# Backward recurrence of a memory-augmented attention: dO of a segment in four column groups over 32 rows, the other 8 rows batched by token tile

## The chip, the cores and the metric

One core of one Trainium2 chip. The metric is the time of one execution on the device in microseconds (us). The kernel before takes 3108.94 us (median of 3 runs, 3106.38 to 3111.91).

## The reference, cut to what matters

A pre-norm block: attention with a recurrent memory, then a gated feed-forward (FFN). The kernel computes the output and nine gradients. The attention works through the 2048 tokens in 64 segments of 32; each segment sees 8 memory rows ahead of its tokens, and the first 8 rows of its output are the memory of the next segment.

```python
M, seg = 8, 32; H, Dh, Dm = 16, 256, 448; n_seg = 2048 // 32
mem = mem0
for s in range(n_seg):
    h = concatenate([mem, x[:, s*seg:(s+1)*seg]])          # 40 rows
    q, k, v = h @ Wq, h @ Wk, h @ Wv                       # 16 heads of 256
    p = softmax(where(mask, q @ k.T * Dh**-0.5, -1e9))
    o = (p @ v) @ Wo                                       # 40 x 448
    mem = o[:, :M]; outs.append(o[:, M:])
```

The backward pass runs through the segments from the last to the first. The gradient of the 8 output rows that became memory comes from the segment handled just before. So for each segment the order is fixed: dO = do x Wo^T (40 rows, 4096 columns), dP = dO x V^T, the softmax gradient dS, the gradients of the heads (dV from P and dO, dK and dQ from dS), their projections back to 448 columns, and the fold that adds the four partial sums and gives the next 8 rows. Of the 40 rows of `do`, only the 8 memory rows wait for the segment before. The change makes two groups of them: 32 rows (the memory rows and 24 token rows) that go through the chain, and the 8 other token rows, which are known long before. Four segments form a token tile of 128 tokens.

Of the kernel before, what the change touches and what calls it, by code (L numbers as in the profile page):

```python
# [812 lines left out]
def ffn_phase(k: _K, back):  # L813
# [32 lines left out]
    for i in range(2):  # L846
        nc.gpsimd.memset(dhb_b[i][:, D:DP], 0.0)
# [88 lines left out]
    for n, gi in enumerate(turns):  # L936
# [67 lines left out]
        for tt in range(G):  # L1004
# [16 lines left out]
            nc.scalar.copy(out=dh_b[:, 0:D], in_=dh_t)  # L1021
            nc.gpsimd.dma_start(out=dr["DHb"][rows, :], in_=dh_b)
# [9 lines left out]
def backward_chain(k: _K):  # L1032
# [9 lines left out]
    WoT_sb = W(0, KC, HD)  # L1042
# [7 lines left out]
    dO_sb = A(52, 16, P)  # L1050
    doT = A(56, 32, 64)
# [5 lines left out]
    P_bd, dS_bd, dST_bd = [B(1.25 * i, 8, 2, L) for i in range(3)]  # L1057
# [13 lines left out]
    def load_seg(s):  # L1071
        if s < NSEG - 1:
            load_v(s)
        for w, (nm, T_sb) in enumerate((("q", Q_sb), ("k", K_sb))):
            t1 = dr["T1"][s, :, w].rearrange("(g x i) n -> g i x n", g=2, x=2)
            t0 = dr["T0" + nm][s // 8].rearrange("(x s i) (g n) -> s g i x n", x=2, s=8, g=2)
            for g in range(2):
                for src, i0, i1 in ((t1[g], M, L), (t0[s % 8, g], 0, M)):
                    k.last_load = nc.sync.dma_start(out=T_sb[64 * g + i0:64 * g + i1].rearrange("p (x c) n -> p x (c n)", x=2), in_=src)
        P_sb = Pb[s % 2]  # L1080
        with tc.issue_after(k.pool_op.ins) if s == NSEG - 1 else nullcontext():
            nc.gpsimd.dma_start(out=P_sb.rearrange("p h n -> p (h n)"), in_=dr["P_all"][s])
        for g in range(2):
            pool_op = nc.gpsimd.tensor_copy(out=P_bd[64 * g:64 * g + L, :, g, :], in_=P_sb[64 * g:64 * g + L, :, :])
        stores("mid", s, pool_op.ins)
# [12 lines left out]
    for tl in (Q_sb, K_sb, P_bd, dS_bd):  # L1098
        nc.gpsimd.memset(tl, 0.0)
    nc.gpsimd.memset(do_roll[:, :, (NSEG - 1) % NWIN, SEG:L], 0.0)  # L1100
    prep_tile(NT - 1)
    load_seg(NSEG - 1)
    load_v(NSEG - 1)
    nc.sync.dma_start(out=WkT_sb[:, 2:MC], in_=dr["Tk"][:, 2:MC])
    yield
    nc.sync.dma_start(out=WoT_sb[:, 0:3, :], in_=dr["To"][:, 0:3, :])
    nc.sync.dma_start(out=WoT_sb[0:64, 3, :], in_=dr["To"][0:64, 3, :])
    nc.gpsimd.memset(WoT_sb[64:P, 3, :], 0.0)
# [5 lines left out]
    nc.vector.memset(doT[:, :, L:64], 0.0)  # L1114
    nc.gpsimd.memset(dST_bd, 0.0)
    nc.gpsimd.memset(dxT[:, KC - 1, :], 0.0)
    om = k.f32("f1", DP, "omb")
    nc.gpsimd.memset(om[:], 0.0)
# [5 lines left out]
    def head_mm(ps, lhs, rhs_bd, turned):  # L1124
        for cl in range(16):
            b, i = divmod(cl, 6)
            at = 8 * (cl // 4 % 2) + 4 * (cl // 8) + cl % 4 if turned else cl
# [3 lines left out]
    for s in range(NSEG - 1, -1, -1):  # L1131
# [7 lines left out]
        if r == 2:  # L1139
            prep_tile(t - 1)  # L1140
        if s < NSEG - 1:
            load_seg(s)

        with k.prio.crit():
            pss = [k.ps1() for _ in range(4)]
            for j in range(MC):
                c = cj(j)
                b, jj = divmod(j, 8)
                for kc in range(KC):
                    with tc.issue_after(k.last_dh.ins) if s == NSEG - 1 and j == 0 and kc == 0 else nullcontext():  # L1150
                        nc.tensor.matmul(pss[b][:, jj * L:(jj + 1) * L], lhsT=WoT_sb[:, kc, c * P:(c + 1) * P],  # L1151
                                         rhs=do_roll[:, kc, sl, :], start=(kc == 0), stop=(kc == KC - 1))
            for b in range(4):
                k.evac(doT[:, 8 * b:8 * b + 8, 0:L], pss[b][:, 0:8 * L].rearrange("p (c n) -> p c n", n=L), "vsvs"[b])

            def token_major(hf):
                ph = k.ps1()[:].bitcast(BF16)
                for i in range(8):
                    c0 = 2 * (8 * hf + i)
                    nc.tensor.transpose(ph[:, i * P:(i + 1) * P], doT[:, c0:c0 + 2, :].rearrange("p c n -> p (c n)"), ident[:, :])  # L1160
                nc.scalar.copy(out=dO_sb[:, 8 * hf:8 * hf + 8, :], in_=ph.rearrange("p (c n) -> p c n", n=P))  # L1161
            token_major(0)
            token_major(1)
            pD = k.ps1()
            for h in range(8):
                for g in range(2):
                    for dc in range(DC):
                        j = 2 * (2 * h + dc) + g
                        nc.tensor.matmul(pD[64 * g:64 * g + 64, h * L:(h + 1) * L], lhsT=doT[:, j, :], rhs=vT[:, 2 * h + dc, L * g:L * g + L],
                                         start=(dc == 0), stop=(dc == DC - 1), skip_group_check=True)  # L1170
# [10 lines left out]
            nc.vector.tensor_tensor(out=dS_bd, in0=prod.unsqueeze(2).to_broadcast([P, 8, 2, L]), in1=P_bd, op=ALU.mult)  # L1181
# [3 lines left out]
            def heads(nm, lhs, rhs):  # L1185
                pps[nm] = [k.ps1() for _ in range(3)]
                head_mm(pps[nm], lhs, rhs, nm != "v")
# [6 lines left out]
                if s == 0:  # L1194
                    k.tl.outs(*{"v": (7, 9), "k": (9, 10), "q": (10, 11)}[nm], 0, 6)
# [7 lines left out]
            heads("v", dO_sb, P_bd)  # L1203
# [12 lines left out]
            rows_in("k", WkT_sb, 20, MC)  # L1216
            rows_in("q", WqT_sb, 0, MC)
            k.last_om = nc.vector.tensor_copy(out=om[:, 0:224], in_=pH[:, 0:224])
            nc.scalar.copy(out=om[:, 224:D], in_=pH[:, 224:D])
            pm = k.ps1()  # L1220
            for kc in range(KC):
                nc.tensor.matmul(pm[:, kc * 32:(kc + 1) * 32], lhsT=om[:, kc * P:(kc + 1) * P], rhs=sel[:],  # L1222
                                 start=True, stop=True)
            pm3 = pm[:, 0:KC * 32].rearrange("p (c m) -> p c m", m=32)
# [291 lines left out]
```

## The kernel before: what the change touches

`k.prio.crit()` marks instructions that belong to the recurrence. The order on each engine is fixed when the program is built: among the instructions that could go, those marked come first, and everything else (from here on: the filler) goes where none of those is ready. `k.ps1()` gives one of five PSUM banks, `k.fx1()` one of two that the filler uses, `k.evac(out, in, "v" or "s")` copies from PSUM on DVE or ACT.

```python
# backward_chain, for s from 63 to 0; t, r = divmod(s, 4)
with k.prio.crit():
    pss = [k.ps1() for _ in range(4)]
    for j in range(MC):                                  # MC = 32 column blocks
        for kc in range(KC):                             # KC = 4, the last padded with zeros
            matmul(pss[b][:, jj*L:(jj+1)*L], lhsT=WoT_sb[:, kc, c*P:(c+1)*P],   # 128 x 128
                   rhs=do_roll[:, kc, sl, :], ...)                              # 40 columns
    for b in range(4): k.evac(doT[:, 8*b:8*b+8, 0:L], pss[b]..., "vsvs"[b])
    token_major(0); token_major(1)                       # 8 transposes and one ACT copy each: dO_sb
    # dP: 32 matmuls, then the softmax gradient on DVE
    nc.vector.scalar_tensor_tensor(out=prod, in0=pD3, scalar=k.scale, in1=P_sb, ...)
    nc.vector.tensor_reduce(out=rsum[:], in_=prod, ...)
    nc.vector.scalar_tensor_tensor(out=prod, in0=pD3, scalar=k.scale, in1=rsum..., ...)
    nc.vector.tensor_tensor(out=dS_bd, in0=prod..., in1=P_bd, op=ALU.mult)
    heads("v", dO_sb, P_bd);  rows_in("v", WvT_sb, 0, MC)   # 16 matmuls of 80 columns; 32 of 448
    heads("k", Q_sb, dS_bd)
    # 16 matmuls that turn dS
    rows_in("k", WkT_sb, 0, 20);  heads("q", K_sb, dST_bd)
    rows_in("k", WkT_sb, 20, MC); rows_in("q", WqT_sb, 0, MC)
    # fold: om = pH; pm = om x sel; do_roll[next] = pm[..., 24:32]
    ...
if r == 0:                                               # once per tile: filler
    px = k.fx1()
    for wi, (nm, WT) in enumerate((("q", WqT_sb), ("k", WkT_sb), ("v", WvT_sb))):
        for j in range(MC): matmul(px[32*(j%4):...], lhsT=lo[nm][:, j, :], rhs=WT[:, cj(j), :], ...)
    # copied, folded into pl = k.fx1(), turned in pX = k.fx1(), layer norm backward, stored
```

## Time and profile before

| stage | stretch (us) | what it is |
|---|---|---|
| forward | 0 to 1055 | not touched |
| FFN backward | 1055 to 1358 | small extra copies only |
| start of the chain | 1358 to 1383 | its first segment, behind a store |
| backward chain | 1383 to 2395 | 63 segments, the change |
| tail | 2395 to 3104 | weight gradients, not touched |

The prediction below shows how the stage is read.

I name a tile's segments r3, r2, r1, r0 in the order in which they run. The four segments between these two copies, from r0 to r1 of the next tile, take 65.46 us. Over the 14 tiles after the first the medians are r3 16.12, r2 16.04, r1 17.04 and r0 15.83, and the tile's is 65.03. The very first tile, which has no filler of an earlier tile beside it, takes 65.05.

### The profile page before, as it was taken

The page shows a single profiled execution, that of the slowest core. Times are in us where ns is not written, and L with a number is a line of the kernel's source. Part 1 is how long each engine was busy: PE and PEld are TensorE (multiplying, and loading weights), DVE is VectorE, ACT ScalarE, POOL GpSimd, SP SyncE. Part 2 cuts the span into 40 slices and gives each one's busy share as a digit, 9 for nine tenths or more (in the row PEclk, how much of TensorE's full clock was granted, in tenths as well). Part 3 has the DMA queues.
Part 4 walks back from the last instruction along what each step waited for, and adds up shares of the span by engine and source line. Part 5 has one row for each costly group of instructions (what it writes and reads, how often), then busy time and mean ns, then how long its engine had stood idle before and what let it go on. Part 6 is the DMA issues. An engine that isn't in the chain of part 4 may idle for free.

```text
span 3103.7 us, 108341 instructions
## 1 busy us (share of the span) xinstructions
PE 2914.8 (94%) x47640; PEld 1735.5 (56%) x47650; DVE 1331.6 (43%) x3381; ACT 1112.6 (36%) x2634; POOL 674.7 (22%) x1511
## 2 busy tenths in 40 slices
PE   5899999989988999989999999999999899999998
PEld 3555555545544555666666666666666454444443
DVE  3555455455455576654444444544445101111110
ACT  2444344344444544443434344444344001111110
POOL 2222222222222222321122111221211111212111
PEclk9999999999999999999999999999999899999999
DMA  6567756756756899984455445555544999969951
GB/s 242 136 172 178 183 162 167 191 158 167 189 161 182 276 222 228 221 298 119 133 150 143 128 137 142 143 139 136 141 138 133 284 267 244 190 181 199 192 160 57
DMA packets 739084, 550.12 MB, mean 177 GB/s; under 512 B 600052, under 2 KB 634852, under 8 KB 736180
## 3 DMA queue, kind: packets, MB, share of 16 engines
q1 hardware_dynamic: 687380, 389.19, 51.5%
q0 software_dynamic: 51232, 154.00, 14.9%
q8 instruction: 374, 6.13, 0.8%
q14 instruction: 98, 0.80, 0.1%
HBM read 168.01 MB, written 234.23 MB: 130 GB/s over the span
## 4 chain that ended last, share of the span: by engine, by line
PE 72%; issue 11%; DVE 6%; DMA 5%; ACT 4%; POOL 2%; SPq 1%; ACTq 0%; POOLq 0%; DVEq 0%
PE po L1200 7%; PE psf L1151 7%; PE psf L535 6%; PE psf L652 5%; PE po L697 4%; PE psf L1375 4%; PE psf L890 4%; PE psf L1128 4%; PE psf L1396 4%; PE fx L1264 3%; PE fx L1014 3%; PE fx L464 2%; PE psf L1222 2%; DVE arA L75 2%; PE psf L549 2%
## 5 line engine op out<-in xcount | busy, mean ns | idle before, releaser
L75 DVE CAST arA<-psf 128x256 bf16<-128x256 f32 (+3 forms) x933 | 427.2, 480 | 808.6 <-PE psf L1375 275.2
L76 ACT CAST arA<-psf 128x96 bf16<-128x96 f32 (+5 forms) x915 | 352.4, 409 | 1036.6 <-PE psf L1375 261.2
L1200 PE MATMUL po<-arW,arA 128*32 128x448 bf16 x6144 | 347.3, 355 | 4.6 <-DMA arW<-Tq 3.5
L1375 PE MATMUL psf<-arW,arA 128*128 128x512 bf16 x980 | 247.1, 380 | 0.0
L1375 PEld LDWEIGHTS <-arA 128*128 128x128 bf16 x1440 | 136.0, 98 | 164.8 <-issue 13.8
L1151 PEld LDWEIGHTS <-arW 128*128 128x128 bf16 x8192 | 213.4, 96 | 25.0 <-issue 25.0
L1151 PE MATMUL psf<-arA,arW 128*128 128x40 bf16 x8192 | 217.0, 180 | 6.2 <-DVE arA L1226 5.1
L652 PE MATMUL psf<-arW,arA 128*64 128x512 bf16 x1536 | 219.0, 386 | 0.0
L1200 PEld LDWEIGHTS <-arA 128*32 128x32 bf16 x6144 | 152.0, 96 | 115.8 <-ACT arA L76 9.4
L535 PE MATMUL psf<-arW,arA 128*32 128x512 bf16 x3072 | 193.8, 385 | 12.5 <-DVE arA L738 12.5
L76 ACT CAST arB<-psf 128x64 bf16<-128x64 f32 (+3 forms) x384 | 121.8, 318 | 153.1 <-PE psf L539 109.7
L697 PE MATMUL po<-arW,arA 128*32 128x256 bf16 (+1 forms) x4096 | 144.2, 267 | 10.5 <-DVE arA L75 7.5
L890 PE MATMUL psf<-arW 128*128 128x256 bf16 (+1 forms) x1288 | 146.3, 274 | 1.3 <-DVE arA L956 0.7
L890 PEld LDWEIGHTS <-arW 128*128 128x128 bf16 (+1 forms) x1344 | 102.4, 97 | 51.4 <-issue 40.8
L1161 ACT COPY arA<-psf 128x1024 bf16<-128x1024 bf16 x128 | 123.3, 1015 | 2.2 <-PE psf L1160 0.4
L1128 PEld LDWEIGHTS <-arW 128*128 128x128 bf16 x2048 | 86.4, 99 | 61.8 <-issue 56.9
L535 PEld LDWEIGHTS <-arA 128*32 128x32 bf16 x3072 | 70.6, 97 | 90.0 <-DVE arA L738 18.1
L76 ACT COPY arA<-psf 128x512 bf16<-128x512 bf16 (+3 forms) x142 | 84.3, 594 | 99.9 <-DVE arA L75 90.3
L464 PE MATMUL fx<-arA,arW 128*128 128x64 bf16 (+1 forms) x2048 | 84.3, 196 | 32.4 <-ACT arB L76 19.2
L697 PEld LDWEIGHTS <-arA 128*32 128x32 bf16 x4096 | 95.9, 98 | 32.9 <-DVE arA L75 10.5
L1128 PE MATMUL psf<-arB,arW 128*128 128x80 bf16 x2048 | 96.8, 201 | 13.6 <-DVE arB L1181 5.2
L1436 POOL DMA_DIRECT2D out_dram<-arA x96 | 51.7, 546 | 249.7 <-DVE arA L75 246.9
(290 smaller groups left out, 4645.7 us busy)
## 6 DMA issues: line engine op xcount, KB each, us to landing
arW<-T SPq DMA_DIRECT2D x256, 128.0 KB
X_o<-arA SPq DMA_DIRECT2D x37, 512.0 KB
T<-arA SPq DMA_DIRECT2D x64, 256.0 KB
X_v<-arA POOLq DMA_DIRECT2D x32, 512.0 KB, 4.9
X_k<-arA POOLq DMA_DIRECT2D x32, 512.0 KB, 4.0
X_q<-arA POOLq DMA_DIRECT2D x32, 512.0 KB, 3.1
out_dram<-arA POOLq DMA_DIRECT2D x90, 128.0 KB, 3.5
VG<-arA SPq DMA_DIRECT2D x64, 160.0 KB
```

What stands on the lines that cost most here:

```text
L75: return nc.vector.tensor_copy(out=out, in_=in_)
L76: return nc.scalar.copy(out=out, in_=in_)
L464: nc.tensor.matmul(banks[w][:, i * 64:(i + 1) * 64], lhsT=lhsT, rhs=xr[lo:hi, kc, :], start=(kc == 0 and i == 0), stop=(kc == KC - 1), ski ...
L535: nc.tensor.matmul(banks[w][32 * q:32 * q + 32, :], lhsT=hT_roll[:, kc, sl, M:L], rhs=(Wq_sb, Wk_sb)[w][:, kc, col(q, b)], start=(kc == 0) ...
L652: nc.tensor.matmul(pV[b][64 * g:64 * g + 64, 0:512], lhsT=hT_flat[:, kc, sl * L:sl * L + 64], rhs=Wv_sb[:, kc, n * 512:(n + 1) * 512], sta ...
L697: nc.tensor.matmul(pO[32 * q:32 * q + 32, 0:w], lhsT=xblk[:, j, r * SEG:(r + 1) * SEG], rhs=Wo_sb[:, cj(j), 256 * dh:256 * dh + w], start= ...
L890: nc.tensor.matmul(ps[fp][:, f2 * 256:(f2 + 1) * 256], lhsT=Wt[lo:hi, kc, c * P:(c + 1) * P], rhs=xT[lo:hi, kc, :], start=(kc == 0 and f2 ...
L1128: nc.tensor.matmul(ps[b][:, i * 2 * L:(i + 1) * 2 * L], lhsT=lhs[:, at, :], rhs=rhs_bd[:, cl // 2, :, :].rearrange("p g n -> p (g n)"), st ...
L1151: nc.tensor.matmul(pss[b][:, jj * L:(jj + 1) * L], lhsT=WoT_sb[:, kc, c * P:(c + 1) * P], rhs=do_roll[:, kc, sl, :], start=(kc == 0), stop ...
L1200: nc.tensor.matmul(pH[32 * (j % 4):32 * (j % 4) + 32, 0:D], lhsT=blk[nm][:, j, r * SEG:(r + 1) * SEG], rhs=WT[:, cj(j), :], start=(nm == " ...
L1375: nc.tensor.matmul(pa[2 * kc + g][:, 0:w], lhsT=lhs_of(b)[:, kc * P:(kc + 1) * P], rhs=rhs_of(b, g), start=(b == 0), stop=(b == nblk - 1), ...
L1396: k.last_mm = nc.tensor.matmul(pa[i][:, 0:D], lhsT=lhs_of(b, i), rhs=rhs_of(b), start=(bi == 0), stop=(bi == len(nblk) - 1))
```

## The change

dO was computed transposed, 40 columns at a time: 128 short matmuls at the floor of about 26 ns each. Now the 32 rows of the chain are the stationary operand, and 512 columns of Wo stream past them, in four groups of 32 array columns at once. dO comes out token-major in two banks and needs 8 transposes instead of 16. The price: Wo's last 64 rows are packed in halves and taken with 64x32 matmuls; P must be laid out by column group (8 matmuls and two DVE products per segment); the V heads (now ahead of dP) take two operands of 160 columns, the second one for the 8 other rows; and those 8 rows are computed for a whole tile in four "units" of 32 matmuls, issued in segments r2 and r1 of the tile handled before, ranked with the chain, each with both filler banks.

```diff
 with k.prio.crit():
-    for j in range(MC):
-        for kc in range(KC):
-            matmul(pss[b][:, jj*L:(jj+1)*L], lhsT=WoT_sb[:, kc, c*P:(c+1)*P], rhs=do_roll[:, kc, sl, :], ...)
-    token_major(0); token_major(1)
+    banks = [k.ps1(), k.ps1()]
+    for b in range(2):
+        for kc in range(KC - 1):
+            for q in range(4):
+                matmul(banks[b][32*q:32*q+32, :], lhsT=do_roll[:, kc, sl, M:L], rhs=WoT_sb[:, kc, col(q, b)], ...)
+        for q in range(4):
+            g, x = divmod(q, 2)
+            matmul(banks[b][32*q:32*q+32, :], lhsT=do_roll[64*x:64*x+64, KC-1, sl, M:L],
+                   rhs=WoT3[64*x:64*x+64, (2*g+b)*512:(2*g+b+1)*512], ...)
+        k.evac(dO_sb[:, b, :], banks[b][:], "vs"[b])
+    turned(0)                       # 4 transposes, evicted into doT
+    values(1)                       # V heads, 8 matmuls: the other 8 rows (dO_rest)
+    turned(1)
+    values(0)                       # V heads, 8 matmuls: the 32 rows (dO_sb)
     ... dP, softmax gradient
-    heads("v", dO_sb, P_bd)
     rows_in("v", WvT_sb, 0, MC)
     ... K heads, Q heads, projections
+    if s > 0: p_by_groups(s - 1)    # 8 matmuls, 2 DVE products with the group mask
     rows_in("q", WqT_sb, 0, MC)
+    if t > 0:
+        for u in {2: (0, 1), 1: (2, 3)}.get(r, ()): rest_unit(t - 1, u)
+        if r == 0: rest_turned(t - 1)
     ... fold
+def rest_unit(t, u):                # 8 other rows of a tile's four segments: 32 columns
+    banks = [k.fx1(), k.fx1()]
+    for kc, i, g, x in ...:         # 32 matmuls
+        matmul(banks[x][:, ...], lhsT=WoT_sb[:, kc, c*P:(c+1)*P],        # kc = 3: 64 rows of WoT3
+               rhs=do_roll[lo:hi, kc, s0:s0+4, 0:M], ...)
```

Cut: buffer addresses, loads, start-up, the fold of the last 64 columns to both halves, evictions of the V heads, the last step of dS in two operations.

## The prediction

> **What bounds the kernel now.** I first read the table of busy time by stretch, to find the stage that the change touches. It is the backward chain: 64 segments, one after the other, each of which needs 8 memory rows from the one before.
>
> ```profile
> 0.00:1055.00 1055.00, 945.81 (x17935) 521.45 (x17936) 542.36 (x1641) 442.00 (x1101) 258.71 (x705) 0.98 0.66 178
> 1055.00:1358.00 303.00, 298.43 (x2278) 183.30 (x2277) 209.67 (x338) 145.17 (x275) 88.91 (x121) 1.00 0.95 252
> 1383.00:2395.00 1012.00, 973.62 (x22959) 696.53 (x22959) 478.39 (x1216) 415.96 (x1082) 198.46 (x458) 1.00 0.50 137
> ```
>
> The columns are the stretch, its length, and busy us of PE, PE weight load, DVE, ACT and POOL. The third row holds 63 segments: 1012 / 63 = 16.06 us each, a third of the kernel. PE looks 96% busy, DVE 47%, the DMA share is 0.50. But the busy figure of PE counts every matmul's whole latency, so it doesn't say whether PE's rate or the order of the dependences sets these 16.06 us. For that I read the chain that ended last through one segment in which PE had almost no other work to put in between:
>
> ```profile
> 2068.86 3.35 PE psf L1151 x128
> 2072.22 0.94 PE psf L1160 x16
> 2073.16 0.64 PE psf L1169 x32
> 2073.80 0.02 issue
> 2073.82 0.49 DVE prod L1176
> 2074.32 0.46 DVE arA L75
> 2074.78 0.39 DVE rsum L1178
> ...
> 2075.18 0.42 DVE arA L75
> 2075.61 0.40 DVE prod L1179
> 2076.01 0.06 DVE arA L75
> ...
> 2076.11 0.84 DVE arB L1181
> ...
> 2077.08 0.39 PE psf L1128 x6
> ...
> 2079.50 0.73 PE psf L1128 x16
> ...
> 2084.90 0.13 PE psf L1151
> ```
>
> Start, length, what. The segment runs from 2068.86 to 2084.90, 16.04 us, in four parts: A, 4.96 us: dO by 128 matmuls, 16 transposes, dP by 32 matmuls. B, 3.26 us: the softmax gradient on DVE, into which three evictions of the V heads (L75: 0.46, 0.42, 0.06) have slipped. C, 2.42 us: K heads and the turning of dS. D, 5.40 us: Q heads, the last projections, the fold to the 8 rows. The segment before, with a dozen and more filler matmuls of L1264 (the memory-row projections of a token tile), took 16.03 us too. So the chain of dependences is the bound, and filler lies free in its gaps.
>
> How near is PE's rate? From the lengths of dense runs in the time order: L1151 128 in 3.30 us (26 ns each), L1160 16 in 0.97 (61), L1169 32 in 0.64, heads 16 in 0.75, L1200 43 in 2.2 (51), turning of dS 0.36, fold (L1222) 1.05. A segment's own work is 3.30 + 0.97 + 0.64 + 3 x 0.75 + 96 x 0.051 (4.9) + 0.36 + 1.05 = 13.5 us. Filler is, per tile of four segments, 96 x 0.051 = 4.9 for L1264 and about 1.8 for folding and turning it: 1.7 per segment. Sum 15.2 of 16.06 us. PE is thus only 0.9 us per segment behind the chain, and this caps the gain.
>
> **What the Trainium skill says.** "TensorE: Matmul & The Clock Gate", Part 3 (Packing small matmuls): outputs at partitions 32j of PSUM land in distinct column groups and run concurrently, three such tiles 2.38 times as fast. The trace agrees: the forward chain's L535 has this very form, and 24 of them take 1.41 us, 59 ns each at 512 columns, where one latency is 385 ns. The same page, Part 1 ("Wait — 56ns, not 53.3ns?"): warm start-to-start is N / 2.4 GHz + 2.5 ns and never below about 25 ns. L1151's 26 ns for 40 columns is that floor, so 40 columns waste it; that is what the change attacks, and the 32-column matmuls that it adds stay on it. "TensorEngine Tiling (Array Packing)", PSUM Bottleneck, warns that eviction may become the limit once tiling has sped up PE. That bears on part A, where eviction of 512 columns is new:
>
> ```profile
> L535 PE MATMUL psf<-arW,arA 128*32 128x512 bf16 x3072 | 193.8, 385 | 12.5 <-DVE arA L738 12.5
> L76 ACT COPY arA<-psf 128x512 bf16<-128x512 bf16 x128 | 74.9, 585 | 88.5 <-DVE arA L75 88.5
> L75 DVE CAST arA<-psf 128x512 bf16<-128x512 f32 x96 | 66.2, 689 | 89.3 <-PE psf L539 87.0 <-PE psf L660 2.1
> L75 DVE COPY arA<-psf 128x512 bf16<-128x512 bf16 x128 | 53.7, 419 | 52.8 <-PE psf L549 52.8
> ```
>
> (Groups of the forward chain: count, busy us, mean ns, idle before.) Evictions to come will cost 0.69 us on DVE from fp32, 0.42 from bf16, 0.585 on ACT.
>
> **The change, part by part: PE work per segment.** dO: out go 128 matmuls (3.30), in come 24 of 128x32 at 59 ns and 8 of 64x32, guessed at 60: 1.89. Transposes: 16 (0.97) become 8 (0.49). V heads: 16 of 80 columns (0.75) become 16 of 160 columns, because P is split by column group and the other 8 rows come from a second operand; 160 / 2.4 + 2.5 = 69 ns by the page's rule, but 80 columns measure 46 against the rule's 36, so I take 75: 1.2. P by groups: 8 in four column groups, 0.2. The other 8 rows: per tile 128 matmuls at the 26 ns floor (3.3) and 8 transposes (0.5), 0.95 per segment. Fold: two more passes, 0.05. Change: -1.41 - 0.48 + 0.45 + 0.2 + 0.95 + 0.05 = -0.24. PE work falls only from 15.2 to 14.95 us: most of what the column groups save is spent again.
>
> The chain of dependences. Part A: dO 1.89; the first half turned (0.25) and half of the V heads (0.6, from the rows known beforehand) cover the ACT eviction of the second half, which ends 1.89 + 0.06 + 0.585 + 0.06 = 2.6 us in; turning the second half until 3.0; its ACT eviction until 3.7 lies beside the other V heads (until 3.6); dP starts there and ends at 4.25. Before: 4.96, gain 0.7. Part B: the V evictions of the high rows start ahead of dP, so 0.46 + 0.42 leave the softmax chain and about 0.2 (low rows) stays; dS becomes two operations of 320 elements, about 0.4 each by L1178/L1179, so the same 0.84. B is 3.26 - 0.75 = 2.5. C and D stay at 2.4 and 5.4, at best. The chain is then about 14.55 us.
>
> Now the two bounds have changed places: the chain would allow 14.55, PE needs 14.95. The gaps in the chain (14.55 less its own PE work of 12.3 = 2.25 us) are smaller than the filler (1.7 + 0.95 = 2.65). No schedule fills gaps fully: with filler to spare, segments before were still at 16.1 for 15.2-15.5 us of work. I add 0.5 us of unfilled time: 15.45 us. Gain 16.06 - 15.45 = 0.6 us, times 63 = 38 us.
>
> Elsewhere: 128 matmuls, evictions and the first P operand (some 6 us) come ahead of the first segment. That segment sits for 11.7 us behind a DMA store (DGP, in the chain of waits at 1367), and I expect the new work to hide there. The extra 64-column copies in the FFN stage (16 x about 0.2 us of ACT) are beside a PE that is 98% busy. P_bd's two POOL copies (0.45 us each) go, a POOL copy of 256 columns comes; POOL is 20% busy. The tail stays.
>
> **The rivals.** First: PE's rate doesn't bind because my dense rates are too high and the packing is good; then the chain's 14.55 to 14.95 decides, and the gain is 1.1 to 1.5 us per segment, 70 to 95 us (3015 to 3040). For it: before, filler was free. Against: 96% PE busy and filler that outgrows the gaps. Second: a tile's filler becomes a chain of its own. L1264's projection, its fold and the 8-row units share two PSUM banks, each unit takes both and waits for its evictions, and the next tile's dP and V heads can't start without the units. L1264's filler took from 2016.6 to 2061, nearly three segments, with gaps of 2.5 us; with smaller gaps it may take four, and the chain then stalls at each tile's boundary by some 3 to 7 us, eating the gain: 3090 to 3110. Third: DVE's order. The new products of P with the group mask are 640 elements from PSUM, 0.82 us each by L1181, twice per segment. If such a one starts just before an operation of the chain, the chain waits, as it does now for the V evictions. Twice 0.5 us would take the chain back to 15.5 and give a gain of 20 to 35 us (3075 to 3090). For it: a DVE that goes from 47% to about 60% of the time. Fourth: the gain is nil because DMA loads set the pace; a DMA share of 0.50 and hardly any wait of the chain on DMA speak against it.
>
> **Range and chances.** My centre is 3108.94 - 38 = 3071 and the first rival pulls a little lower: 3069. The range goes from nearly full packing (15.0 us per segment, -67 us) to most of the gain lost (15.9, -10): 3042 to 3098. More than 2% needs 62 us, or 15.07 us per segment, only 0.12 above the PE work I count; I give it 0.22. Slower by 2% would need stalls of 5 us per tile on top of no gain: 0.03.
>
> **What would show it right or wrong.** In the new profile the chain should run at about 15.4 us per segment with PE busy still at 95% or more; the dO matmuls should take about 1.9 us per segment, and the time from the first dO matmul to the end of dP 4.2 to 4.5; the softmax part 2.3 to 2.6; DVE near 60%. Filler that still runs in every segment, with the last segment of a tile no shorter than the others, would confirm PE's rate as the bound. It is wrong if segments take 15.0 us or less (packing better than I hold possible), if the first segment of each tile is several us longer than the others (second rival), or if the DVE products of P stand in the chain that ended last (third).

## More of the kernel before

One view is added here, since it measures every kernel that follows: each segment ends with one small DVE copy (L1226) that writes the 8 rows for the next, so the distance of two such copies is the length of a segment. They are from the time order of DVE in the kernel before, over one token tile; the columns are start, length, engine, line, operation, and in brackets the idle time before it and what ended it.

```profile
2003.15 0.19 DVE L1226 CAST arA<-psf 128x32 bf16<-128x32 f32 x1 [1.58 <-PE psf L1222]
...
2068.61 0.19 DVE L1226 CAST arA<-psf 128x32 bf16<-128x32 f32 x1 [1.58 <-PE psf L1222]
```

## The result, and the profile after

After: 3137.72 us (median of 4 runs, 3135.56 to 3150.49), beside 3109.4 for the kernel before (4 runs). A ratio in this document is the mean time of one kernel's fast runs over that of the other's of the same rounds, so not quite the ratio of the medians. Here it is 1.010, 95% interval 1.0072 to 1.0129: slower by 1%. The prediction said 3069 and a range of 3042 to 3098. Both are missed, and the direction is wrong.

The chain again, by the table of busy time (stretch, length, busy PE, PE weight load, DVE, ACT, POOL, granted clock, DMA share, GB/s):

```profile
1383.00:2395.00 1012.00, 965.38 (x18455) 611.64 (x18448) 580.22 (x1365) 328.66 (x1053) 163.88 (x383) 0.99 0.49 131
```

The end of the stage is now at 2432.4 instead of 2394.5: first to last copy is 1049.9 us against 1011.6, so the stage lost 38.3 us, of which the whole kernel shows 28. (The tail begins with a load that it waits for anyway: 36.2 us from the last copy to its first matmul before, 30.5 after.) Copies of that kind, after:

```profile
2006.06 0.19 DVE L1336 CAST arA<-psf 128x32 bf16<-128x32 f32 x1 [1.68 <-PE psf L1332]
2023.09 0.19 DVE L1336 CAST arA<-psf 128x32 bf16<-128x32 f32 x1 [0.45 <-PE psf L1332]
2042.93 0.19 DVE L1336 CAST arA<-psf 128x32 bf16<-128x32 f32 x1 [1.32 <-PE psf L1332]
...
2073.99 0.19 DVE L1336 CAST arA<-psf 128x32 bf16<-128x32 f32 x1 [1.68 <-PE psf L1332]
```

The first two distances are r1, 17.03, and r0, 19.84; the four segments together take 67.93. The medians over the 14 tiles after the first:

| kernel | r3 | r2 | r1 | r0 | tile, median | tile, mean |
|---|---|---|---|---|---|---|
| before | 16.12 | 16.04 | 17.04 | 15.83 | 65.03 | 65.25 |
| after | 15.19 | 15.59 | 17.03 | 19.85 | 67.75 | 68.21 |

So the change did work: two segments are 0.45 and 0.9 us shorter. r0 alone lost 4 us. The first tile, with units but without filler, takes 62.71, 2.3 us less than before.

Why r0 is long is seen in the chain that ended last. First an ordinary segment, r3:

```profile
2043.38 0.65 PE psf L1216 x12
...
2048.16 0.50 DVE prod L1270
...
2050.86 0.73 PE psf L1192 x16
...
2053.28 0.73 PE psf L1192 x16
...
2058.85 0.65 PE psf L1216 x12
```

L1216 is the start of dO (24 matmuls of L1216 and 8 of L1220 make a segment's), L1270 the first DVE step behind dP, L1192 the K and then the Q heads, and the last line is the next segment's dO. The four parts of the prediction are A 4.78 us (2043.38 to 2048.16), B 2.70, C 2.42 and D 5.57; predicted were 4.25, 2.5, 2.4 and 5.4. Now r0 of the same tile, from the start of dO:

```profile
2024.00 0.76 PE psf L1216 x12
...
2025.08 0.59 PE fx L1109 x16
...
2026.53 0.59 PE fx L1109 x16
...
2027.98 0.89 PE fx L1109 x32
...
2029.60 0.79 PE fx L1109 x32
...
2032.44 0.48 DVE prod L1270
```

96 matmuls of the units (L1109) lie inside dO and the V heads: 0.59 + 0.59 + 0.89 + 0.79 = 2.86 us. Part A is 8.44 us (2024.00 to 2032.44) instead of 4.78. And dO itself, cut in seven pieces, takes 3.11 us (0.76 + 0.32 + 0.32 + 0.53 + 0.54 + 0.32 + 0.32 in the chain) instead of 2.07 (the chain counts a piece from the end of the one before it). The cut itself costs: one 64x32 matmul alone takes 0.32 us in this chain, as long as three of them here or four in r3 (0.33), so a group of four that is cut takes the time of two groups, besides the changes of tile form (measured below).

In the same segment PE then sits idle for 1.09 us, waiting for the last step of dS (L1276), with no filler left to put there. The same wait stands in every segment: its median is 0.6 to 0.65 us in r3, r2 and r1, where more filler does follow later, and 1.17 in r0. These are the groups of the K and Q heads in this stage, after and then before (count, busy us, mean ns, idle before them and what ended it).

```profile
L1192 PE MATMUL psf<-arB,arW 128*128 128x80 bf16 x1904 | 87.3, 200 | 45.3 <-DVE arB L1276 41.2
```

```profile
L1128 PE MATMUL psf<-arB,arW 128*128 128x80 bf16 x1984 | 93.8, 201 | 13.1 <-DVE arB L1181 4.9 <-DMA arB<-XN 0.3
```

After, PE is idle for 46.6 us of the 1012 (1012.00 - 965.38), and 45.3 of these lie here, nearly all in part B. Everywhere else it is busy in the records. Work was moved into A (the V heads) and D (folds, units), and B was left with too little. But the kernel before was idle for 38.4 us (1012.00 - 973.62), only in more places. Idle time has gathered in B more than it has grown, and most of the 38 us is not idle PE.

### The profile page after: what moved, and what is told of

It reads as the page before. It is cut to its first block, busy times and chain, and to the rows that moved or that the text cites. A ratio compares the mean times of both kernels' runs of the same rounds, so it can differ in the third digit from the quotient of the medians.

```text
span 3133.8 us, 100710 instructions
## 1 busy us (share of the span) xinstructions
PE 2942.5 (94%) x43810; PEld 1671.4 (53%) x43810; DVE 1459.8 (47%) x3588; ACT 1039.3 (33%) x2666; POOL 640.8 (20%) x1457
## 4 chain that ended last, share of the span: by engine, by line
PE 69%; issue 11%; DVE 9%; DMA 5%; ACT 3%; POOL 2%; SPq 0%; ACTq 0%; POOLq 0%; DVEq 0%
PE psf L535 6%; PE po L1301 5%; PE psf L652 5%; PE po L697 4%; PE psf L1485 4%; PE psf L1506 4%; PE psf L888 4%; PE psf L1216 3%; PE fx L1012 3%; PE psf L1192 2%; PE psf L1240 2%; PE fx L464 2%; DVE arA L75 2%; PE fx L1374 2%; PE psf L549 2%
## 5 line engine op out<-in xcount | busy, mean ns | idle before, releaser
L75 DVE CAST arA<-psf 128x256 bf16<-128x256 f32 (+4 forms) x805 | 374.4, 500 | 803.0 <-PE psf L1485 275.2
L76 ACT CAST arA<-psf 128x512 bf16<-128x512 f32 (+3 forms) x915 | 349.3, 422 | 1022.1 <-PE psf L1485 261.2
L1301 PE MATMUL po<-arW,arA 128*32 128x448 bf16 x6144 | 357.0, 354 | 3.1 <-DVE arA L75 3.1
L1301 PEld LDWEIGHTS <-arA 128*32 128x32 bf16 x6144 | 169.4, 96 | 100.2 <-DVE arA L75 7.4
L535 PE MATMUL psf<-arW,arA 128*32 128x512 bf16 x3072 | 193.8, 385 | 12.5 <-DVE arA L738 12.5
L76 ACT COPY arA<-psf 128x512 bf16<-128x512 bf16 (+3 forms) x222 | 131.4, 592 | 132.2 <-DVE arA L75 92.7
L1192 PE MATMUL psf<-arB,arW 128*128 128x80 bf16 x2048 | 93.9, 200 | 49.2 <-DVE arB L1276 44.7
L75 DVE COPY arA<-psf 128x512 bf16<-128x512 bf16 (+2 forms) x220 | 93.9, 427 | 94.6 <-PE psf L549 53.0
L1192 PEld LDWEIGHTS <-arW 128*128 128x128 bf16 x2048 | 84.4, 98 | 97.2 <-issue 85.0
L888 PEld LDWEIGHTS <-arW 128*128 128x128 bf16 (+1 forms) x1344 | 102.4, 97 | 52.8 <-issue 41.9
L535 PEld LDWEIGHTS <-arA 128*32 128x32 bf16 x3072 | 70.5, 96 | 90.2 <-DVE arA L738 18.1
L1216 PE MATMUL psf<-arW,arA 128*32 128x512 bf16 x1536 | 116.8, 397 | 0.4 <-DVE arA L1336 0.3
L697 PEld LDWEIGHTS <-arA 128*32 128x32 bf16 x4096 | 94.5, 97 | 32.0 <-DVE arA L75 10.6
L464 PEld LDWEIGHTS <-arW 128*128 128x128 bf16 (+1 forms) x2048 | 70.6, 98 | 54.3 <-issue 32.9
```

The lines of the kernel that those rows point to most:

```text
L75: return nc.vector.tensor_copy(out=out, in_=in_)
L76: return nc.scalar.copy(out=out, in_=in_)
L464: nc.tensor.matmul(banks[w][:, i * 64:(i + 1) * 64], lhsT=lhsT, rhs=xr[lo:hi, kc, :], start=(kc == 0 and i == 0), stop=(kc == KC - 1), ski ...
L535: nc.tensor.matmul(banks[w][32 * q:32 * q + 32, :], lhsT=hT_roll[:, kc, sl, M:L], rhs=(Wq_sb, Wk_sb)[w][:, kc, col(q, b)], start=(kc == 0) ...
L697: nc.tensor.matmul(pO[32 * q:32 * q + 32, 0:w], lhsT=xblk[:, j, r * SEG:(r + 1) * SEG], rhs=Wo_sb[:, cj(j), 256 * dh:256 * dh + w], start= ...
L888: nc.tensor.matmul(ps[fp][:, f2 * 256:(f2 + 1) * 256], lhsT=Wt[lo:hi, kc, c * P:(c + 1) * P], rhs=xT[lo:hi, kc, :], start=(kc == 0 and f2 ...
```

## The experiments

Theory at the start: PE's work sets the tile now, and the units are what it can't afford: they need both filler banks, which the filler holds until the middle of r1, so that they come late, and, ranked with the chain, then go into dO. Rivals: the rank alone is at fault; the DVE products of P; the evictions in part A or the order of its steps; the layer norm of the tile on DVE. In all tables "tile" is the median over the 14 tiles after the first, read as above in the one execution of each kernel that was profiled; the time is the median of all its executions.

**The kernel after again (e8).** No edit. The same chip as e5 to e7.

> The changed kernel itself, unchanged, as the control on this chip: 3130 to 3150, 0.7 to 1.3% over the kernel before, in every theory.

3146.28 us, ratio 1.0112 (1.0085 to 1.0138), tile 67.67. The loss repeats.

**Without the units (e1).** Wrong: only the units of the first two tiles are computed, and turned.

```diff
-            if t > 0:
+            if t == NT - 1:
                 for u in {2: (0, 1), 1: (2, 3)}.get(r, ()): rest_unit(t - 1, u)
```

> The 8-row units (128 matmuls per token tile) are computed for the first two tiles only and reused for all others; the result is wrong on purpose. Everything else is the changed kernel. In its trace a tile of four segments takes 67.7 us against 65.0 before, and the two segments in which the units run take 17.0 and 19.85 us against 15.2 to 15.6 of the two others. Theory 1 (the units rank with the chain, so they are run in front of dO and the fold as soon as their two PSUM banks are free, instead of in the gaps): a tile falls to about 62.5 to 63, 15 tiles times 4.7 to 5 us, total 3062 to 3070. Rival A (PE's rate is the bound, units cost their bare PE time of 3.5 us per tile): 3080 to 3090. Rival B (the products of P on DVE are what lengthens the chain): above 3125.

3064.46 us, ratio 0.9834 (0.978 to 0.9888). The tile is 62.6 (15.25, 15.65, 16.45, 15.24).

**With hardly any filler (e5), and with a third of it (e13).** The memory-row projections L1374 are cut from 96 matmuls per tile to 4, and to 32. The outputs are then within tolerance, but something that belongs to the result is missing.

```diff
-            for wi, (nm, WT) in enumerate((("q", WqT_sb), ("k", WkT_sb), ("v", WvT_sb))):
-                for j in range(MC):
+            for wi, (nm, WT) in enumerate((("q", WqT_sb),)):
+                for j in range(4):          # e13: range(MC)
```

> The changed kernel with the filler cut down: of the 96 matmuls per token tile that project the memory rows only 4 are left (wrong on purpose); the 8-row units stay, with their rank in the chain. In the kernel before this filler cost nothing. Theory 1, now sharpened (the gaps of the shorter chain hold only about one filler, 1.7 us per segment, and the units come on top of it): the order of instructions shows the units moving into the gaps of three segments, so a tile falls from 67.7 to 61 to 62.5 us as in the first tile, which has no such filler (62.7), total 3040 to 3065; the saving of 5 to 6.5 us per tile is more than the 4.7 us that the removed matmuls take. Rival C (the units cost by their rank, wherever they land): they still cost 4 to 5 us, a tile stays at 66 to 68, 3115 to 3140.

> The changed kernel with 32 of the 96 filler matmuls per tile (wrong on purpose), units as they were. The order shows the units now starting in the tile's third segment and partly in gaps. Theory 1 (gaps hold one filler): between the 61.3 us per tile without filler and 67.7 with all of it, 62 to 64, total 3055 to 3085. If the units' cost came from their rank alone: 66 to 68, 3120 to 3145.

e5: 3039.25 us, ratio 0.9771 (0.9749 to 0.9793), tile 61.27. e13: 3073.47 us, ratio 0.9897 (0.9875 to 0.9919), tile 63.26. Where the units go in e5 is seen in its chain of waits:

```profile
2016.67 0.24 PE fx L1109 x10
...
2017.61 0.52 PE fx L1109 x15
2018.13 0.76 PE psf L1216 x12
```

They stand around the fold and its evictions, where PE has gaps, and dO that follows is whole: with the banks free, the units are not late. The four cells of this comparison are 62.6 with filler alone, 61.3 with units (nearly) alone, 67.7 with both, and the one with neither, which comes next. Beside the other, each costs 5 to 6 us: the units 67.7 - 62.6 = 5.1, the filler 67.7 - 61.3 = 6.4. Taking 64 filler matmuls away (3.3 us of PE by the prediction's 0.051 each) saves 4.5 us per tile, the next 28 (1.4 us) 2.0: about what PE spends and somewhat more, and at neither dose was the filler free, as all of it was before. Beside the units, PE's time sets the tile.

**With neither (e9).** The edits of e1 and e5 together, wrong.

> Wrong on purpose: neither the 8-row units (after the first two tiles) nor the memory-row filler. With the runs before it completes a square: tile median 67.7 us with both, 62.6 with the filler alone, 61.3 with the units alone. Theory 1 (the gaps hold one of the two nearly free, not both): the bare chain takes 60.5 to 61.3 us per tile, so that each alone costs 0 to 2 us and both together over 6; total 3020 to 3040. Rival C (each costs about its own PE time wherever it is): 56 to 58 us per tile, total under 2985.

3060.15 us, ratio 0.985 (0.981 to 0.989), tile 63.97: longer than with the units alone, and above the 3020 to 3040 that were expected. (The profiled execution was the slowest of the four, 3080.62; the others took 3058.99 to 3060.34.) The tile of this cell doesn't measure the floor, because the clock was no longer granted in full. Its busy table for the middle of the stage, and for 7 us of it:

```profile
1440.00:2340.00 900.00, 793.38 (x14366) 503.91 (x14367) 526.85 (x1230) 298.77 (x937) 154.48 (x365) 0.96 0.50 140
2009.00:2016.00 7.00, 6.64 (x64) 3.38 (x64) 1.31 (x3) 1.40 (x6) 1.21 (x3) 0.76 0.68 188
```

The granted clock is the third number from the right. In the chain of waits twelve dO matmuls took 1.25 and 1.40 us within these 7 us, instead of 0.65 to 0.76. A kernel from which work is taken away to find its floor must be read together with the clock. In single segments it can be: those of e9 over which the clock was granted in full have medians of 15.57 (r3), 15.04, 15.03 and 15.95 (r0), from 5 to 13 segments each, together 61.6 us. That fills the fourth cell. Each load alone costs 1.0 us (filler, 62.6) or nothing (units, 61.3), and both together 6.1. The gaps hold one of them, not both.

**The rank (e2).** The same units, outside the block that is ranked with the chain.

```diff
-            if t > 0:
-                for u in {2: (0, 1), 1: (2, 3)}.get(r, ()): rest_unit(t - 1, u)
-                if r == 0: rest_turned(t - 1)
+            if t > 0 and r == 0: rest_turned(t - 1)
...
+        if t > 0:                            # after the ranked block
+            for u in {2: (0, 1), 1: (2, 3)}.get(r, ()): rest_unit(t - 1, u)
```

> Same work and right result, but the four 8-row units are issued outside the chain's priority block, so that they rank as filler behind the chain. The order of instructions shows 69 of the 128 unit matmuls now in gaps of the tile's last segment and 59 still in front of the V heads of the next tile's first segment, which needs them. Theory 1: about half of the 4.7 us per tile comes back, 3095 to 3115, near the kernel before. Rival A (PE's rate): no change, 3130 to 3140. Rival B: no change.

3156.16 us, ratio 1.0134 (1.0088 to 1.0179), correct, tile 68.94, where a gain was expected. r0 is short now (15.91) and the next tile's first segment takes 20.07. Nine of these 14 tiles contain a stretch in which the clock was halved (see below); the five others have a median of 67.65, and the first segment takes 19.51 at full clock. In the kernel after, the tiles at full clock take 67.66. So the rank moves the stall and leaves the tile as it was. Its chain of waits there:

```profile
1988.20 0.64 PE fx L1109 x24
...
1989.34 0.29 DVE arW L75
1989.67 0.60 PE fx L1109 x14
```

The V heads wait for 59 matmuls of the units, for the evictions between two of them (the shared banks; L75 is one) and for the turning L1120. This is the stall at the tile's boundary that the second rival named; the rank in the change avoids it and pays in r0 instead. Rank isn't the cause.

**The DVE products of P (e3).** Wrong: P by groups only for the first segment.

```diff
-            if s > 0:
-                p_by_groups(s - 1)
```

> P by column groups (8 matmuls and two DVE products of 0.82 us per segment) is computed once for the first segment and reused; the result is wrong on purpose. Rival B (these products stand in the chain): 0.8 to 1.6 us per segment come off, 3040 to 3090. Theory 1: only the 0.2 us of PE time per segment or less, 3120 to 3135.

3142.54 us, ratio 1.0091 (1.0046 to 1.0137), tile 67.16, mean 68.25 (after 67.75 and 68.21). By the medians 0.15 us per segment at most (0.12 by the tiles at full clock, 67.16 and 67.66), by the means nothing; neither expected range was met. The third rival, at 0.8 to 1.6 us per segment, falls.

**Evictions and order in part A (e4, e10, e11, e12).** e4 splits the second half's two evictions over DVE and ACT. e12 puts dP ahead of all V heads, as the kernel before had it; e10 and e11 do so on e7 and e6 below.

```diff
 e4
-                k.evac(dO_sb[:, b, :], banks[b][:], "vs"[b])
+                for hf in range(1 + b):      # b = 1: two halves, on DVE and ACT; doT likewise
+                    c0, c1 = (256*hf, 256*hf + 256) if b else (0, 512)
+                    k.evac(dO_sb[:, b, c0:c1], banks[b][:, c0:c1], "vs"[hf])
 e12 (e10, e11: on top of e7, e6, with the units' evictions on ACT)
             turned(0)
-            values(1)
             turned(1)
-            values(0); evictions "svs"
             ... dP, softmax gradient
+            values(1); values(0); evictions "sss"
```

> Right result. The two evictions on ACT that part A of a segment waits for (second half of dO, second half of the turned dO, 0.59 us each) are split between DVE and ACT. If these evictions set part A, which measured 4.8 us against the 4.25 predicted, 0.2 to 0.45 us per segment come off: 3108 to 3125. If PE's own order sets it (V heads until just before dP), less than 0.1 us per segment: 3131 to 3138.

> Right result. Column-group units ranked as filler, and besides dP is placed ahead of the V heads in the chain, with the V evictions and the units' evictions on ACT. Part A then no longer contains the 16 matmuls of the V heads (1.3 us), only the waits for two evictions, into which filler goes. If the V heads in front of dP are what made part A 4.8 instead of 4.25 us: A 4.0 to 4.3, B up to 0.3 longer, tile 63.3 to 64.6, total 3070 to 3095. If PE's rate is the bound now (59.7 us of work per tile and gaps too short to fill), the tile stays at 65 to 66: 3100 to 3115.

> The same with the units ranked with the chain. Tile 63.5 to 65, total 3070 to 3100, if the order of dP and V heads counts; 3105 to 3115 if not.

> The changed kernel with its 128-matmul units as they were, and only dP placed ahead of the V heads with the V evictions on ACT. If part A's order counts by itself: 0.3 to 0.5 us per segment off the changed kernel, 3110 to 3127. If not: 3135 to 3150.

| kernel | us | ratio (95%) | tile |
|---|---|---|---|
| e4 | 3156.27 | 1.0136 (1.0084 to 1.0188) | 68.53 |
| e10 | 3121.19 | 1.0031 (0.9993 to 1.0068) | 65.87 |
| e11 | 3118.68 | 1.0043 (0.9996 to 1.0091) | 66.61 |
| e12 | 3160.71 | 1.0158 (1.0129 to 1.0187) | 69.02 |

All correct, and none has a better total than its base (the kernel after, e7, e6 and the kernel after; tiles 67.75, 65.95, 65.53, 67.75). All four came out even slower than was expected for the case of no effect; why e4 and e12 lengthen the tile by about 1 us was not looked into. In e10 the V heads fill part B, but B grows: its chain of waits from the end of dP on:

```profile
2047.81 0.94 PE psf L1235 x12
...
2051.13 0.33 PE psf L1187 x6
```

Between the V heads (L1235) and the K heads (L1187) lies PE work without a gap (filler 0.30 and 0.19, projections 0.47 and 1.41): B is 3.3 us instead of 2.7, and what A gained is given back. In none of these orders was the segment shorter.

**Cheaper units (e6, e7).** The 8 rows of a tile's four segments are 32 rows, so they can be computed as dO is: 32 rows stationary, 512 columns streamed. Two units of 16 matmuls per tile, one bank each, instead of four of 32 with two. e6 ranks them with the chain, e7 does not.

```diff
-    banks = [k.fx1(), k.fx1()]
-    ... 32 matmuls of 32 columns, 4 units per tile
+    bank = k.fx1()
+    for kc in range(KC):
+        for q in range(4):
+            matmul(bank[32*q:32*q+32, :], lhsT=xr[t][lo:hi, kc, :], rhs=WoT_sb[:, kc, col(q, b)], ...)   # kc = 3: WoT3
-            for u in {2: (0, 1), 1: (2, 3)}...
+            for u in {3: (0,), 2: (1,)}...
```

> Right result. The 8 other rows of a token tile are computed by four column groups as well, from a packed copy of 32 rows: 32 matmuls of 512 columns into one PSUM bank at a time, instead of 128 of 32 columns into two banks at once; the turned form then comes from 8 transposes as before. Same rank in the chain. PE time per tile 3.7 -> 2.1 us, and the order shows both units in the fold of the tile's third segment, none within dO. Theory 1: the units' cost falls from 5.1 to 2 to 2.5 us per tile, tile 64.6 to 65.3, total 3092 to 3105, about the kernel before.

> As the run with column-group units, but ranked as filler. The order shows all 32 unit matmuls and their transposes in the gaps of the last segment, done before the next tile needs them, unlike the 128 small ones. Theory 1: the units cost 0 to 1.5 us per tile, tile 62.6 to 64.2, total 3065 to 3090, faster than the kernel before by 0.6 to 1.4%. If PE's rate is the bound (rival A): tile above 64.6, 3095 or more.

e6: 3109.39 us, ratio 1.0 (0.9969 to 1.003), tile 65.53 (15.19, 15.59, 17.63, 17.12). e7: 3110.85 us, ratio 1.0002 (0.9982 to 1.0023), tile 65.95. Both correct. Making the units cheap and keeping them out of dO takes back the whole loss, and the rank hardly matters. It gains nothing over the kernel before. These runs change the units' cost, their banks and their place at once, and don't tell how much each is worth. e7 had been expected at 3065 to 3090; a tile above 64.6 had been named as the sign that PE's rate is the bound, and it came.

**The layer norm (e14, e15, e16).** In e6 the chain of waits of r0 led through the layer norm of the tile on DVE (a dO eviction stood behind it in the fixed order of DVE). e14, e15 and e16 put its last step on POOL, on the kernel after, e6 and e7.

```diff
-        nc.vector.tensor_tensor(out=out_ap, in0=t1[:, c0:c1], in1=resid_ap, op=ALU.add)      # in this stage only
+        nc.gpsimd.tensor_tensor(out=out_ap, in0=t1[:, c0:c1], in1=resid_ap, op=ALU.add)
```

> The changed kernel, right result, with the last addition of the layer-norm backward in the chain's stage (two of 224 columns per tile) on POOL instead of DVE. Theory 1: PE is in order and busy throughout dO of that segment, so nothing changes, 67.2 to 67.8 us per tile, 3135 to 3150. Theory 2 (DVE's queue behind the layer norm is what lengthens that segment): 1 to 2 us per tile less, 3108 to 3130.

> Right result. Column-group units ranked with the chain, and the addition on POOL. Here the chain does go through the layer norm: the last segment falls from 17.1 to 15.5 to 16.2 us, the tile from 65.5 to 64.0 to 64.7, total 3080 to 3098, 0.3 to 0.9% faster than the kernel before. If another wait takes its place: 3100 to 3112.

> Right result. The same with the units ranked as filler: tile 64.3 to 65.2 from 65.9, total 3085 to 3105; no change (3105 to 3115) if the units' eviction ahead of the head evictions is what costs there.

e14: 3138.28 us, 1.0113 (1.0086 to 1.0141), tile 67.66. e15: 3102.49 us, 0.999 (0.9964 to 1.0017), tile 65.14. e16: 3128.0 us, 1.0065 (1.0045 to 1.0085), tile 67.09. All correct. In the kernel after the layer norm isn't it; in e6 it was worth 0.4 us per tile; in e7 the step on POOL made the median worse by 1.1 us per tile. Most of that is the clock: seven of the 14 tiles of e16 contain a stretch at half clock and take 67.8 to 68.2 us, the seven others have a median of 66.40. Why those are still 0.45 above e7's is not known.

**The form of the array (e17, e18).** Left over was dO itself: predicted 1.89 us per segment. The Trainium skill, "TensorEngine Tiling (Array Packing)", Key Properties, says that a change of the tiling mode, not just of the tile, drains TensorE. I hadn't used this. dO changes from 128x32 to 64x32, back, and to 64x32 again before it leaves for the transposes. e17 gives the last quarter all 128 rows, with the same number of matmuls; they then sum two column blocks, so dO is wrong. e18 is the same on e15.

```diff
-    matmul(banks[b][32*q:32*q+32, :], lhsT=do_roll[64*x:64*x+64, KC-1, sl, M:L], rhs=WoT3[64*x:64*x+64, cols], ...)
+    matmul(banks[b][32*q:32*q+32, :], lhsT=do_roll[:, KC-1, sl, M:L], rhs=WoT3[:, cols], ...)
```

> The kernel after with one edit, wrong on purpose: the last 8 matmuls of dO take all 128 rows (128x32) instead of 64 (64x32), so that dO keeps one tile form. They then sum two column blocks and dO is wrong; the number of matmuls stays. In the kernel after four 64x32 matmuls took 0.33 us (82 ns each) behind twelve 128x32 in 0.65 to 0.76 us. If the change of form costs PE a drain, four of them fall to about 0.25 us, dO of a segment from 2.07-2.18 us to about 1.9-2.0, and as PE's work sets the tile, a tile falls by 0.7 to 1 us (67.7 to about 66.8) and the total by 10 to 15 us, to 3124 to 3130. If the form change costs nothing and the work does not set the tile, both stay (3138).

> The same edit on the kernel of e15 (units as 32 matmuls of 128x32 and 64x32 ranked with the chain, end of the layer norm on POOL), wrong on purpose in the same way. Drain theory: 65.14 us per tile falls to about 64.4, the total from 3102 to about 3090. If not, 3102.

e17: 3115.63 us, ratio 1.0034 (1.0011 to 1.0058), tile 66.10 (14.88, 15.27, 16.71, 19.11). e18: 3089.41 us, ratio 0.9945 (0.992 to 0.9971), tile 64.19 (14.87, 15.27, 17.31, 16.74). PE's time order, the kernel after and then e17 (start and length; a length here includes the latency of the last matmul, so the rate is read from the starts):

```profile
1717.58 0.82 PE L1216 MATMUL psf<-arW,arA 128*32 128x512 bf16 x12
1718.33 0.40 PE L1220 MATMUL psf<-arW,arA 64*32 64x512 bf16 x4
1718.65 0.83 PE L1216 MATMUL psf<-arW,arA 128*32 128x512 bf16 x12
...
1719.74 0.40 PE L1228 MATMUL psf<-ident,arA 128*128 128x128 bf16 x4
```

```profile
1712.85 0.82 PE L1216 MATMUL psf<-arW,arA 128*32 128x512 bf16 x12
1713.49 0.39 PE L1220 MATMUL psf<-arW,arA 128*32 128x512 bf16 x4
1713.71 0.82 PE L1216 MATMUL psf<-arW,arA 128*32 128x512 bf16 x12
...
1714.70 0.40 PE L1228 MATMUL psf<-ident,arA 128*128 128x128 bf16 x4
```

From start to start: twelve and then four are 0.75 and 0.32 with the change of form, 0.64 and 0.22 without it. Each of the three changes that went is worth about 0.11 us. The whole dO is 2.16 us against 1.85. Every segment without a unit in its dO became 0.32 us shorter, one to one (r3 15.19 to 14.88, r2 15.59 to 15.27, r1 17.03 to 16.71; first tile 14.96 to 14.64). I had expected 0.7 to 1 us per tile from e17; it was 1.65, since I had not counted the change back, and since r0 gained 0.74. There dO is cut by units, another form, and changes more often, which is argued and was not taken apart. e18 beats the kernel before by 0.55%, but with a wrong dO. A correct kernel of that speed would need the last quarter's stationary operand masked with zeros, one copy for each half; that costs a small copy per segment. Nothing correct that I ran beats the kernel before.

**The clock, in passing.** The kernel after has a mean tile 0.46 us above its median. In five of 13 tiles of the stretch 1450 to 2340 the first twelve dO matmuls of r0 took 1.47 us instead of 0.82. The busy table just before and in such a place:

```profile
1950.60:1954.02 3.42, 3.42 (x47) 2.73 (x39) 1.28 (x3) 0.56 (x3) 0.00 (x0) 1.00 0.20 50
1954.02:1957.44 3.42, 3.42 (x39) 1.73 (x36) 1.01 (x5) 1.21 (x6) 0.21 (x1) 0.50 0.00 0
```

The granted clock, third from the right, falls to half for 3.42 us, right after 3.42 us that hold the last projections (until 1951.15) and then only folds, one fp32 transpose and sixteen unit matmuls of 32 columns, although PE never was idle there; at the same place of the next tile it stays at 1.00. Between 1395 and 2345 us, the clock records of e8 and e14 show four such falls each, e13 five, e17 six, e3 four longer ones, e4 two, e12 three, e2 eleven and e9 twenty-one; e1 (no units), e5 (hardly any filler), e6, e11, e15, e18 and the kernel before show none. Units of 512 columns do not exclude it: e7 has two, e10 one and e16 seven. What brings it on stays open. In the kernel after it explains some 0.46 x 14 = 6.4 us of the 38, an estimate from mean less median. The tiles that it touches can be told apart: the nine at full clock have a median of 67.66, the five others take 68.8 to 70.0.

## Why the prediction was wrong, point by point

**What bounds the kernel before.** Right: the chain does, filler is free (65.05 without it, 65.03 with it). Right too: after the change the two bounds have changed places, and beside the units PE's time sets the tile (e1, e5, e13). But its bare work alone does not: that work is 61.6 us per tile, as counted below, the tile with neither load is 61.6 too (e9), and the tile with both is 6 us above either. The caution drawn from it, to trust only 38 us, did not go far enough.

**PE's work, "14.95 us".** Too low by 0.45. The price of 59 ns for a dO matmul was right: e17's 1.85 us for 32 is 58 each. What failed is the line "8 of 64x32, guessed at 60": they are 82 ns each in place, and the change of form costs 0.11 us three times, 2.16 us instead of 1.89. The kernel before shows this pair already, in its forward chain:

```profile
500.40 1.48 PE L535 MATMUL psf<-arW,arA 128*32 128x512 bf16 x24 [0.27 <-DVE arA L738]
501.81 0.41 PE L539 MATMUL psf<-arW,arA 64*32 64x512 bf16 x8
502.15 1.48 PE L535 MATMUL psf<-arW,arA 128*32 128x512 bf16 x24
```

In the trace, four of these start within 10 ns of one another and the next four 0.216 us later, 54 ns each. Six groups are 1.30 us; the 1.41 from L535 to L539, and so the 59 ns, hold one change of form.

The units are 0.49 + 0.49 around the fold and 2.86 within r0, 3.84 us per tile instead of 3.3. Added up from the traces as in the prediction, a segment holds dO 2.16, transposes 0.67, V heads 1.12, dP 0.64, projections 4.9, K and Q heads 1.46, dS turned 0.32, P by groups 0.21, fold 1.14: 12.62. A tile is four of these, the filler 6.7 and the units with their turning 4.4 (3.84 + 0.55): 61.6 us, or 15.4 per segment.

**"I add 0.5 us of unfilled time: 15.45 us".** This is the step that failed most. The tile is 67.75, so that 6.15 us, 1.54 per segment, are not filled. Of these some 3.1 us per tile are idle PE, nearly all in part B (46.6 us of 1012, times 67.75); the rest is PE that is busy in the records but not at its rate: the cuts and changes of form in r0's dO (3.11 - 2.07 = 1.04 us per tile) are the part I can name. An estimate agrees: seven pieces are eleven rounds of four column groups instead of eight, at 0.21 us each (0.64 / 3 in e17), and four changes of form more, at 0.11: 1.07. About 2 us per tile stay without a name. Together, per segment: 15.45 + 0.45 (more work) + 1.04 (1.54 - 0.5, more unfilled time) = 16.94 = 67.75 / 4. The 0.5 was taken from a kernel whose filler could go anywhere. After the change part of the filler is tied: units to banks that come free in r1, and to V heads that need them in the next tile, so they go where they must and not where PE is idle. How much of the unfilled time each of these two ties costs is not measured.

**The chain, "14.55 us".** Nearly right. Where no filler is in the way (first tile, second segment) it takes 14.96, and 14.64 in e17, without the change of form. A was 4.78 instead of 4.25 (0.3 of it the change of form; the rest lies around the eviction before dP, 0.59 us of ACT, which the V heads did not cover), B 2.70 instead of 2.5: 0.94 us of evictions left the softmax part and it gained only 0.56. Its DVE steps counted for 0.39 to 0.40 us each with an eviction in between; now that each follows directly on the step whose result it needs, they count for 0.50, and dS in two operations takes 0.98 instead of 0.84. The time order of DVE, before and then after:

```profile
2040.93 0.49 DVE L1176 SCALAR_TENSOR_TENSOR prod<-psf,arB 128x320 f32<-128x320 f32 x1 [1.91 <-PE psf L1169]
2041.33 0.55 DVE L75 CAST arA<-psf 128x384 bf16<-128x384 f32 x1
```

```profile
2048.16 0.49 DVE L1270 SCALAR_TENSOR_TENSOR prod<-psf,arB 128x320 f32<-128x320 f32 x1 [0.25 <-PE psf L1263]
2048.69 0.49 DVE L1272 TENSOR_REDUCE rsum<-prod 128x8 f32<-128x320 f32 x1
```

The eviction (L75) needs nothing from L1176 and starts 0.40 us after it; L1272 needs L1270's result and starts 0.53 us after it; the steps that follow start 0.52 us after one another. That the need for the result is the reason is not shown: of the evictions behind L1178 in the kernel before, which need nothing of it, 33 of 47 start over 0.50 us after it as well (2042.31 after 2041.80 in this segment).

**The rivals.** The second was the right one in kind: filler and units share two banks, units come late, and the chain pays. Its place was wrong (inside r0's dO, since the units are ranked with the chain; at the boundary only in e2), and its range, 3090 to 3110, too low. The first (good packing, 3015 to 3040) fell: the dO matmuls run at the rate hoped for, but the rest of PE's work rose. The third (DVE products) fell with e3. The fourth (DMA) was given no support: the DMA share stayed at 0.49.

**The rest.** Right: start-up work hid (first copy at 1382.53, before 1382.88); DVE is 57% busy in the stage (580 of 1012; "near 60%"); PE is 95% busy; dO takes "about 1.9 us" only without the change of form. The sign that was to prove me wrong, a segment of a tile several us longer than the others, is what came, in r0.

What stays open: what exactly holds e18's r1 and r0 at 17.3 and 16.7 us when r3 takes 14.9. Folding of the filler (1.02 us), its fp32 transposes and a unit (1.09 us) stand in them, but I have not taken these away one by one. The tile without filler and units is known only as a sum of single segments at full clock (61.6), and still holds the folding and the turning of the filler.

## What to carry to other kernels

Before moving work off a chain, count PE's whole work with its changes of tile form, and ask of every piece of new filler not only how long it takes but when it can start and by when it must be done: filler that is tied to banks and to a deadline lands in the chain, even beside idle gaps. When two parts of a change each cost little alone, run the square of with and without; here it showed that the loss comes from two loads on one engine, each nearly free alone. And read the clock of any run from which work was taken away, before its time is called a floor; where the clock falls only in places, compare the tiles that it leaves alone.

## What the Trainium skill lacked or had wrong

- "TensorEngine Tiling (Array Packing)", Key Properties, says that a change of tiling mode drains TensorE, and gives no size. Here, between 128x32 and 64x32 matmuls of 512 columns, a change cost 0.11 us: 0.32 and 0.75 us against 0.22 and 0.64 (after against e17).
- "TensorE: Matmul & The Clock Gate", Part 1, ties the throttle to how busy PE was and gives as the practical rule that there should be no idle gap of more than about 3.4 us. Keeping that rule was not enough here: the granted clock fell to 0.50 for 3.42 us right after 3.42 us in which the records show PE busy throughout, most of it with fp32 folds and matmuls of 32 columns. In e9 the mean granted clock was 0.96 over 900 us with PE 88% busy. Why is open.
